# Scaling the scores of heads 0 to 7 in the exponential instead of scaling q

## The chip, the cores and the metric

The kernel runs on one core of a Trainium2 chip. The metric is the device time of one execution in microseconds (us). The engines are TensorE (PE in the rows, its weight loads PEld), VectorE (DVE), ScalarE (ACT), GpSimd (POOL) and SyncE (SP, whose queue issues the transfers here).

## What is computed

Attention over 4 batches of 8 heads (576 tokens, head width 64, causal by blocks of 64 tokens), and two feed-forward layers (width 512, inner width 2048) on its output:

```python
scores = scale * np.matmul(q, k.transpose(0, 1, 3, 2))      # scale = 1 / sqrt(64)
scores = np.where(mask, scores, -1000000000.0)
scores = scores - np.max(scores, axis=-1, keepdims=True)
attn = np.exp(scores)
attn = attn / (np.sum(attn, axis=-1, keepdims=True) + 1e-09)
x = np.matmul(attn, v)
...
h = x @ w_in;  g = np.maximum(0.01 * h, h);  x = g @ w_out
h = x @ w2_in;  g = P(h) / (Q(h) + 1e-06);  out = g @ w2_out
```

## The kernel before

The 32 heads are worked through one by one in one loop. The first eight (`NSF = WHOLE = 8`, the first batch) take plain 32-bit matmuls; from head 8 on q, k, the probabilities and v are split into a high and a low part. While a batch's heads are computed, matmuls of the first layer for the batch before are filled in between (`moe1`), so during heads 0 to 7 there are none; TensorE then has only the heads' own work. Beside all this the weights are converted block by block (`convert`): a block `cs` is loaded by SP, ScalarE (line 174) and GpSimd (178, for the first nine blocks) take its halves apart, VectorE (196) joins them, ScalarE (199) rounds a high part and GpSimd (200) subtracts it.

One head has a row of steps, in an order given by a string (`ORDERS` for head 0, `ORDER0` for heads 1 to 8). Their parts, with lines of the profile:

- Step 1 calls `a1(n + 1)`: for heads 1 to 7 ScalarE multiplies the next head's q (tile `fq`, 64 x 576) by the scale in place (line 272 through the helper at 262).
- Steps x, y, z call `a2_part`: TensorE computes the scores of one or two of the head's five row tiles (308), VectorE takes each row's negated maximum into `nm` (320), ScalarE takes the exponentials with that maximum as bias and the row sums as a second output (326). x is the last row tile (576 keys), y has those of 448 and 320 keys, z those of 192 and 64. Behind the last of them `a2_norm` adds a small number to the sums, takes reciprocals (332, 333) and normalises the five tiles (336, on VectorE in these heads).
- Steps a and b transpose the normalised tiles of the head before (363) and copy them out of PSUM, by ScalarE or VectorE (346).
- Step 4 multiplies the transposed tiles of head n - 2 with v (391, 395); ScalarE casts the result to a high part `xh` (402), VectorE subtracts (403) and copies the last 64 columns (404).

Scores, transposes and products all use one PSUM pool of four buffers (tile `T`), so a matmul group often waits for an exponential or a copy that empties a buffer. The tiles of q and k, and those of the probabilities (`PB`, five for even heads, five for odd ones), are reused too.

Head 0 is an exception already before the change: its q isn't scaled; its maxima are (324), and its exponential has the scale as a factor.

The order of the instructions on SP is the order of the code. On the other engines a scheduler of the framework sets it, by costs of its own, so an instruction less or more can move others. Each engine then works strictly in that order.

Of the kernel before, what the change touches and what calls it, by code (L numbers as in the profile page):

```python
# [14 lines left out]
AF = mybir.ActivationFunctionType  # L15
# [10 lines left out]
def attention_moe_moe_kernel(  # L26
# [15 lines left out]
    B, H, D, S = q.shape  # L42
# [8 lines left out]
    SCALE = 1.0 / float(D) ** 0.5  # L51
# [39 lines left out]
    plain = [  # L91
        [ap.tile([P, S], F32, tag=f"{nm}{j}", name=f"{nm}{j}") for nm in ("fq", "fk")] for j in range(4)
    ]
# [4 lines left out]
    PB = [[ap.tile([P, P * (i + 1)], F32, name=f"PB{e}{i}") for i in range(5)] for e in range(2)]  # L98
# [29 lines left out]
    NSF = 8  # L128
# [105 lines left out]
    def split_tiles(n):  # L234
        e, j = n % 2, (2 * n - NSF) % 4
        for d, nm, i in ((QT, "fq", j), (KH, "fk", j), (QM, "fq", j + 1), (KL, "fk", j + 1)):
            d[e] = ap.tile([P, S], F32R, tag=f"{nm}{i % 4}", name=f"split_{nm}{i % 4}")
        for c, d in enumerate((QM, KL)):
            src = plain[(NSF - 1) % 4][c] if n == NSF else d[1 - e].bitcast(F32)
            cp1("p", d[e][D:P, :], src[D:P, :])  # L240
# [19 lines left out]
    def cp1(eng, out, in_, by=1.0):  # L260
        if eng == "a":
            nc.scalar.activation(out, in_, AF.Copy, scale=by)
        elif eng == "v":
            nc.vector.tensor_scalar(out, in_, by, None, ALU.mult)
        else:
            nc.gpsimd.tensor_scalar(out, in_, by, 1.0, ALU.mult, ALU.mult)

    def a1(n):
        if n < NSF:
            if n > 0:  # L270
                fq = plain[n % 4][0][0:D, :]
                cp1("a", fq, fq, SCALE)
            return
        if n < NSF + 2:
            split_tiles(n)
        e = n % 2
        qs, ks = qk[e][0:D, :], qk[e][D:P, :]
        cp1(E1[0], QT[e][0:D, :], qs, SCALE)
        nc.vector.scalar_tensor_tensor(
            QT[e][D:P, :], qs, SCALE, QT[e][0:D, :].bitcast(F32), ALU.mult, ALU.subtract  # L280
        )
        cp1(E1[2], QM[e][0:D, :], QT[e][0:D, :].bitcast(F32))
        cp1(E1[3], KH[e][D:P, :], ks)
        cp1(E1[4], KH[e][0:D, :], ks)
        (nc.gpsimd if n < NSF + 3 else nc.vector).tensor_tensor(
            KL[e][0:D, :], ks, KH[e][D:P, :].bitcast(F32), ALU.subtract
        )
# [9 lines left out]
    def a2_part(n, tiles, st):  # L297
        e = n % 2
        nm, sm = st
        done = []  # L300
        T = psA.tile([P, 1024], F32, tag="A", name="T")
        for o, i in tiles:
            ln = KEYS[i]
            parts = [(o, 0, max(ln, P))] if i < 4 else [(512 - NH2, 0, NH2), (512, NH2, NH2)]
            for po, c, w in parts:
                if n < NSF:
                    fq, fk = plain[n % 4]
                    nc.tensor.matmul(  # L308
                        T[:, po:po + w], lhsT=fq[:, FIRST[i]:FIRST[i] + P], rhs=fk[:, c:c + w],
                        start=True, stop=True,  # L310
                    )
                    continue
                for lhs, rhs in ((QT, KH), (QM, KL)):
                    nc.tensor.matmul(  # L314
                        T[:, po:po + w], lhsT=lhs[e][:, FIRST[i]:FIRST[i] + P], rhs=rhs[e][:, c:c + w],
                        start=(lhs is QT), stop=(lhs is QM),
                    )
            done.append((i, ln, T[:, parts[0][0]:parts[0][0] + ln]))
        for i, ln, sc in done:
            nc.vector.tensor_reduce(nm[:, i:i + 1], sc, axis=AX.X, op=ALU.max, negate=True)  # L320
        idx = [i for i, _, _ in done]
        c = slice(min(idx), max(idx) + 1)
        if n == 0:
            nc.vector.tensor_scalar(nm[:, c], nm[:, c], SCALE, None, ALU.mult)
        for i, ln, sc in done:
            nc.scalar.activation(  # L326
                PB[e][i][:, 0:ln], sc, AF.Exp, scale=SCALE if n == 0 else 1.0, bias=nm[:, i:i + 1], accum_out=sm[:, i:i + 1]
            )

    def a2_norm(n, sm):  # L330
# [338 lines left out]
    with tc.manual_schedule(engines={mybir.EngineType.SP}):  # L669
# [51 lines left out]
        for n, (b, h) in enumerate(heads):  # L721
# [3 lines left out]
            nm = cp.tile([P, 5], F32, tag="nm", name="nm")  # L725
            sm = cp.tile([P, 5], F32, tag="sm", name="sm")
# [3 lines left out]
            for step, f in zip(steps, fills):  # L730
                if step == "1" and n + 1 < NHD:
                    a1(n + 1)
                elif step == "v":
                    if n >= WHOLE:
                        a1v(n)
                    if n < WHOLE and odd:
                        load_v(p + 1)
                elif step == "4":
                    save_left()
                    apply(n - 2)  # L740
                elif step == "x":
                    a2_part(n, [(0, 4)], (nm, sm))
                elif step == "y":
                    a2_part(n, [(0, 3), (512, 2)], (nm, sm))
                elif step == "z":
                    a2_part(n, [(0, 1), (512, 0)], (nm, sm))
                elif step == "a" and n > 0:
                    if n >= WHOLE and odd and p < NHD // 2 - 1:
                        load_v(p + 1)
                    a3a(n - 1)  # L750
                elif step == "b" and n > 0:
                    a3b(n - 1)
                if step == max("xyz", key=steps.index):
                    a2_norm(n, sm)
                fill(f)
                pace(n, steps.index(step) + 1)
# [90 lines left out]
```

## Time and profile before

| | |
|---|---|
| median of three runs | 1027.13 us (1027.13 to 1029.51) |
| the profiled execution's own time | 1031.21 us |
| its span, first to last instruction | 1029.3 us |
| busy: TensorE, VectorE, ScalarE, GpSimd | 96%, 71%, 65%, 26% of the span |
| granted TensorE clock, mean | 0.991 |

The span is a little shorter than the execution, which also holds what lies before the first and after the last instruction. Busy shares are averages over very different stages: the heads come first, then what is left of the first layer, then the second layer with TensorE at work all the time. A matmul's end is modelled, so a busy TensorE may still be waiting inside.

### The profile page before, as it was taken

The numbers are of one execution on the slowest core, as the hardware profiler recorded it, in microseconds if no ns is written. First come the engines' busy times: TensorE is split into PE (matmuls) and PEld (weight loads), VectorE is DVE, ScalarE is ACT, GpSimd is POOL, SyncE is SP. The second block draws the span as 40 slices with busy tenths as digits, with TensorE's granted clock in tenths as the row PEclk, the third lists the DMA queues.
The fourth block names the chain that finished last, engine by engine and source line by source line (L and its number), as shares of the span: only waits on it lengthen the run. The fifth ranks groups of instructions, "written<-read, shape, count | busy, mean of one in ns | idle before, by whom it ended". The sixth has DMA issues, their size and how long they took to land.

```text
span 1029.3 us, 14577 instructions
## 1 busy us (share of the span) xinstructions
PE 991.0 (96%) x4968; PEld 828.4 (80%) x4968; DVE 731.4 (71%) x1270; ACT 672.8 (65%) x1371; POOL 272.6 (26%) x333
## 2 busy tenths in 40 slices
PE   6989989898999999999999999999999999999997
PEld 4667777787888888888888898888888888888886
DVE  4797767676676676665333234999888888888885
ACT  5778877766566766665554334876766776676675
POOL 5256656554444563532331211000000000000000
PEclk8999999999999999999999999999999999999999
DMA  6457959546454574542865686602102000110010
GB/s 181 134 162 257 305 175 288 184 163 211 128 169 148 161 240 127 177 139 78 280 199 183 209 293 236 254 1 82 42 1 82 21 22 4 37 41 1 1 42 21
DMA packets 94762, 140.95 MB, mean 137 GB/s; under 512 B 10336, under 2 KB 47200, under 8 KB 94688
## 3 DMA queue, kind: packets, MB, share of 16 engines
q1 hardware_dynamic: 94688, 140.02, 42.3%
q8 instruction: 39, 0.64, 0.3%
q14 instruction: 35, 0.29, 0.1%
HBM read 108.53 MB, written 31.46 MB: 136 GB/s over the span
## 4 chain that ended last, share of the span: by engine, by line
PE 77%; ACT 7%; DVE 6%; DMA 5%; issue 3%; POOL 2%; SPq 1%; DVEq 0%; ACTq 0%; POOLq 0%
PE M L480 29%; PE h L581 19%; PE o L635 19%; PE T L363 3%; DMA cs<-in_moe_w_in_dram 3%; PE T L395 3%; PE T L314 2%; ACT PB L326 2%; PE T L308 1%; DVE nm L320 1%; ACT cs L174 1%; DMA xld<-vr 1%; DVE PB L336 1%; DVE pTl L356 1%; ACT cs L180 1%
## 5 line engine op out<-in xcount | busy, mean ns | idle before, releaser
L480 PE MATMUL M<-gh,w1o 128*128 128x512 f32 (+1 forms) x320 | 120.4, 377 | 5.7 <-ACT PB L326 3.2
L480 PE MATMUL M<-gl,w1o 128*128 128x512 f32 (+1 forms) x320 | 120.2, 376 | 0.0
L480 PE MATMUL M<-gh,wl 128*128 128x512 f32 (+1 forms) x320 | 119.3, 373 | 0.0
L326 ACT ACTIVATE PB<-T,nm 128x448 f32<-128x448 f32 (+4 forms) x160 | 83.1, 524 | 43.7 <-DVE nm L320 40.7
L593 ACT ACTIVATE ea<-h,coef 128x512 f32<-128x512 f32 (+1 forms) x80 | 51.7, 646 | 90.8 <-PE h L581 90.7
L490 DVE TENSOR_TENSOR gl<-M,gh 128x512 fp32r<-128x512 f32 (+1 forms) x80 | 50.5, 632 | 68.6 <-ACT M L489 68.6
L581 PE MATMUL h<-x2h,w2h 128*128 128x512 f32 (+1 forms) x240 | 88.3, 368 | 0.5 <-DVE acc L497 0.5
L581 PE MATMUL h<-x2h,w2l 128*128 128x512 f32 (+1 forms) x240 | 88.3, 368 | 0.0
L581 PE MATMUL h<-x2l,w2h 128*128 128x512 f32 (+1 forms) x240 | 88.3, 368 | 0.0
L635 PE MATMUL o<-w2h,g2h 128*128 128x512 f32 x216 | 84.2, 390 | 0.0
L635 PE MATMUL o<-w2l,g2h 128*128 128x512 f32 x216 | 84.2, 390 | 0.0
L635 PE MATMUL o<-w2h,g2l 128*128 128x512 f32 x216 | 84.0, 389 | 0.0
L336 POOL TENSOR_SCALAR PB<-PB,sm 128x448 f32<-128x448 f32 (+4 forms) x120 | 69.9, 604 | 48.9 <-DVE sm L333 48.9
L320 DVE TENSOR_REDUCE nm<-T 128x1 f32<-128x448 f32 (+4 forms) x160 | 71.6, 479 | 14.0 <-PE T L308 10.6
L174 ACT ACTIVATE cs<-cs 128x512 f32<-128x512 f32 x64 | 43.1, 674 | 57.2 <-DMA cs<-in_moe_w_in_dram 36.3
L596 DVE SCALAR_TENSOR_TENSOR ea<-eh,coef,ea 128x512 f32<-128x512 f32 (+1 forms) x80 | 55.7, 696 | 33.5 <-ACT eh L594 32.7
L363 PE MATMUL T<-ident,PB 128*128 128x128 f32 x480 | 67.8, 282 | 10.6 <-ACT PB L326 6.6
L480 PE MATMUL M<-xh,w1i 128*128 128x512 f32 x256 | 74.6, 402 | 2.0 <-ACT xh L412 1.1
L363 PEld LDWEIGHTS T<-ident,PB 128*128 128x128 f32 x480 | 56.9, 145 | 23.4 <-ACT PB L326 5.6
L196 DVE SCALAR_TENSOR_TENSOR cl<-cs 128x512 int32<-128x512 int32 x64 | 52.4, 822 | 31.9 <-ACT cs L180 23.9
L480 PEld LDWEIGHTS M<-gh,w1o 128*128 128x128 f32 x320 | 60.6, 190 | 15.8 <-ACT PB L326 3.9
L480 PE MATMUL M<-xh,wl 128*128 128x512 f32 x256 | 73.0, 401 | 0.0
(128 smaller groups left out, 2533.5 us busy)
## 6 DMA issues: line engine op xcount, KB each, us to landing
wl<-w1l SPq DMA_DIRECT2D x160, 256.0 KB, 2.9
cs<-in_moe_w_in_dram SPq DMA_DIRECT2D x32, 512.0 KB, 5.3
cs<-in_moe_w_out_dram SPq DMA_DIRECT2D x32, 512.0 KB, 5.5
w1l<-cl SPq DMA_DIRECT2D x32, 256.0 KB, 4.9
vr<-in_v_dram SPq DMA_DIRECT2D x16, 256.0 KB, 3.4
w2h<-ch SPq DMA_DIRECT2D x16, 256.0 KB, 3.7
w2l<-cl SPq DMA_DIRECT2D x16, 256.0 KB, 3.9
x2hd<-xo SPq DMA_DIRECT2D x16, 256.0 KB, 2.7
```

What stands on the lines that cost most here:

```text
L174: nc.scalar.activation(hi.bitcast(F32), hi.bitcast(F32), AF.Prelu, scale=2.0 ** -112, alpha=-(2.0 ** 32))
L196: nc.vector.scalar_tensor_tensor(f.bitcast(I32), hi, 3, lo, ALU.logical_shift_left, ALU.bitwise_or)
L320: nc.vector.tensor_reduce(nm[:, i:i + 1], sc, axis=AX.X, op=ALU.max, negate=True)
L326: nc.scalar.activation(PB[e][i][:, 0:ln], sc, AF.Exp, scale=SCALE if n == 0 else 1.0, bias=nm[:, i:i + 1], accum_out=sm[:, i:i + 1])
L336: (nc.vector if n < WHOLE else nc.gpsimd).tensor_scalar(PB[e][i][:, 0:ln], PB[e][i][:, 0:ln], sm[:, i:i + 1], 1.0, ALU.mult, ALU.mult)
L363: nc.tensor.transpose(T[:, c:c + P], PB[e][i][:, kt * P:(kt + 1) * P], ident)
L480: nc.tensor.matmul(T, lhsT=w[:, kk, :], rhs=A[kk][lo], start=(m == 0), stop=(m == 11))
L490: nc.vector.tensor_tensor(gl, T, gh.bitcast(F32), ALU.subtract)
L581: nc.tensor.matmul(h[:, 0:n], lhsT=a, rhs=x, start=(kk == 0 and i == 0), stop=(kk == KD - 1 and i == 2))
L593: nc.scalar.activation(a, h, AF.Abs, scale=coef[:, 4:5])
L596: nc.vector.scalar_tensor_tensor(a, h2, coef[:, 5:6], a, ALU.mult, ALU.add)
L635: nc.tensor.matmul(ob[t], lhsT=a, rhs=w, start=(f == 0 and i == 0), stop=(f == NF - 1 and i == 2))
```

## The change

Heads 1 to 7 are treated as head 0 was: q is left unscaled, the maxima are multiplied by the scale, and the exponential multiplies the scores by it.

```diff
     def a1(n):
         if n < NSF:
-            if n > 0:
-                fq = plain[n % 4][0][0:D, :]
-                cp1("a", fq, fq, SCALE)
             return
...
         c = slice(min(idx), max(idx) + 1)
-        if n == 0:
+        if n < NSF:
             nc.vector.tensor_scalar(nm[:, c], nm[:, c], SCALE, None, ALU.mult)
         for i, ln, sc in done:
             nc.scalar.activation(
-                PB[e][i][:, 0:ln], sc, AF.Exp, scale=SCALE if n == 0 else 1.0, bias=nm[:, i:i + 1], accum_out=sm[:, i:i + 1]
+                PB[e][i][:, 0:ln], sc, AF.Exp, scale=SCALE if n < NSF else 1.0, bias=nm[:, i:i + 1], accum_out=sm[:, i:i + 1]
             )
```

Line numbers behind the first place are lower by three in the changed kernel (326 is 323, 402 is 399). In the rows below `PB_103` to `PB_107` are the five probability tiles of an even head and `PB_108` to `PB_112` those of an odd one, in the order of their row tiles (64, 192, 320, 448, 576 keys).

ScalarE at the start of the program, before:

```order
L670 ACT_TABLE_LOAD
L262 ACTIVATE fq_95<-fq_95 64x576
L262 ACTIVATE fq_97<-fq_97 64x576
L174 ACTIVATE cs<-cs 128x512
L262 ACTIVATE fq_99<-fq_99 64x576
L326 ACTIVATE PB_106,sm<-T,nm 128x448
L326 ACTIVATE PB_105,sm<-T,nm 128x320
L326 ACTIVATE PB_104,sm<-T,nm 128x192
L326 ACTIVATE PB_103,sm<-T,nm 128x64
L326 ACTIVATE PB_107,sm<-T,nm 128x576
L326 ACTIVATE PB_112,sm<-T,nm 128x576
L174 ACTIVATE cs<-cs 128x512
```

The same place with the change:

```order
L667 ACT_TABLE_LOAD
L174 ACTIVATE cs<-cs 128x512
L323 ACTIVATE PB_106,sm<-T,nm 128x448
L323 ACTIVATE PB_105,sm<-T,nm 128x320
L323 ACTIVATE PB_104,sm<-T,nm 128x192
L323 ACTIVATE PB_103,sm<-T,nm 128x64
L323 ACTIVATE PB_107,sm<-T,nm 128x576
L174 ACTIVATE cs<-cs 128x512
L323 ACTIVATE PB_112,sm<-T,nm 128x576
L199 CAST w1i<-cl 128x4x128
L174 ACTIVATE cs<-cs 128x512
L323 ACTIVATE PB_111,sm<-T,nm 128x448
```

The three scalings of q are gone, and the second weight block now stands ahead of head 1's first exponential (`PB_112`).

ScalarE in head 5, before:

```order
L326 ACTIVATE PB_112,sm<-T,nm 128x576
L326 ACTIVATE PB_111,sm<-T,nm 128x448
L326 ACTIVATE PB_110,sm<-T,nm 128x320
L402 CAST xh<-T 64x512
L346 COPY acc<-T 128x896
```

The same place with the change:

```order
L323 ACTIVATE PB_112,sm<-T,nm 128x576
L199 CAST w1o<-cl 128x4x128
L399 CAST xh<-T 64x512
L323 ACTIVATE PB_111,sm<-T,nm 128x448
L323 ACTIVATE PB_110,sm<-T,nm 128x320
L343 COPY acc<-T 128x896
```

The cast of the product with v (`xh`, of head 3) moved ahead of two exponentials; the same happens in head 2.

VectorE at the first maxima of head 6, before:

```order
L336 TENSOR_SCALAR PB_110<-PB_110,sm 128x320
L320 TENSOR_REDUCE nm<-T 128x1 x2
L279 SCALAR_TENSOR_TENSOR split_fq_647<-qk_89,split_fq_647 64x576
L196 SCALAR_TENSOR_TENSOR cl<-cs 128x512
L403 TENSOR_TENSOR xl<-T,xh 64x512
```

The same place with the change:

```order
L333 TENSOR_SCALAR PB_110<-PB_110,sm 128x320
L321 TENSOR_SCALAR nm<-nm 128x1
L317 TENSOR_REDUCE nm<-T 128x1 x2
L276 SCALAR_TENSOR_TENSOR split_fq_658<-qk_89,split_fq_658 64x576
L321 TENSOR_SCALAR nm<-nm 128x2
L196 SCALAR_TENSOR_TENSOR cl<-cs 128x512
```

The two rows of line 321 are new. The first, for x, stands behind the normalisation of head 5 (line 333); the second, for y, behind the split of q for head 8 (line 276).

## Rows read from the trace of the kernel before

**Rows 1.** The page, 40 slices of the span: granted TensorE clock, in tenths.

```profile
PEclk8999999999999999999999999999999999999999
```

**Rows 2.** Chain that ended last, 0 to 260 us: start, us, what.

```profile
30.65 0.68 DVE xl L403
...
44.28 0.60 ACT fq L262
...
55.11 0.59 ACT xh L402
55.71 0.92 ACT acc L346
```

**Rows 3.** Timeline of ScalarE: start, us, instruction, [idle before <-releaser].

```profile
9.32 0.67 ACT L174 ACTIVATE cs<-cs 128x512 f32<-128x512 f32 x1 [1.95 <-DMA cs<-in_moe_w_in_dram]
12.08 0.68 ACT L262 ACTIVATE fq<-fq 64x576 f32<-64x576 f32 x1 [2.09 <-DMA fq<-in_q_dram]
12.67 0.61 ACT L326 ACTIVATE PB<-T,nm 128x448 f32<-128x448 f32 x1
...
13.28 0.51 ACT L326 ACTIVATE PB<-T,nm 128x320 f32<-128x320 f32 x1
...
14.47 0.74 ACT L326 ACTIVATE PB<-T,nm 128x576 f32<-128x576 f32 x1
...
15.19 0.74 ACT L326 ACTIVATE PB<-T,nm 128x576 f32<-128x576 f32 x1
...
43.60 0.68 ACT L174 ACTIVATE cs<-cs 128x512 f32<-128x512 f32 x1 [1.48 <-DMA cs<-in_moe_w_in_dram]
44.19 0.69 ACT L262 ACTIVATE fq<-fq 64x576 f32<-64x576 f32 x1
44.78 0.62 ACT L326 ACTIVATE PB<-T,nm 128x448 f32<-128x448 f32 x1
```

**Rows 4.** Timeline of VectorE.

```profile
8.87 0.16 DVE L324 TENSOR_SCALAR nm<-nm 128x2 f32<-128x2 f32 x1
8.94 0.22 DVE L320 TENSOR_REDUCE nm<-T 128x1 f32<-128x64 f32 x1
...
11.57 0.15 DVE L324 TENSOR_SCALAR nm<-nm 128x1 f32<-128x1 f32 x1
...
33.86 1.57 DVE L336 TENSOR_SCALAR PB<-PB,sm 128x448 f32<-128x448 f32 x5
...
43.20 1.02 DVE L320 TENSOR_REDUCE nm<-T 128x1 f32<-128x448 f32 x2
...
59.59 3.84 DVE L336 TENSOR_SCALAR PB<-PB,sm 128x448 f32<-128x448 f32 x5
...
64.40 0.75 DVE L279 SCALAR_TENSOR_TENSOR split_fq<-qk,split_fq 64x576 fp32r<-64x576 f32 x1
```

**Rows 5.** Timeline of TensorE.

```profile
4.59 6.57 PE L308 MATMUL T<-fk,fq 128*128 128x448 f32 x16 [4.59 <-POOL fk L229]
13.94 2.93 PE L308 MATMUL T<-fk,fq 128*128 128x448 f32 x4 [2.77 <-ACT PB L326]
...
23.11 2.58 PE L308 MATMUL T<-fk,fq 128*128 128x288 f32 x8
...
25.76 2.75 PE L395 MATMUL T<-acc,vr 128*128 128x448 f32 x10
```

**Rows 6.** Stages: length, busy PE, PEld, DVE, ACT, POOL, then PEclk, DMA share, GB/s.

```profile
12.00:14.00 2.00, 0.06 (x1) 0.06 (x1) 0.39 (x1) 1.92 (x6) 0.00 (x0) 0.80 1.09 241
...
23.50:24.00 0.50, 0.50 (x3) 0.38 (x2) 0.50 (x2) 0.30 (x1) 0.12 (x1) 1.00 0.52 86
...
70.00:80.00 10.00, 8.95 (x50) 6.78 (x48) 9.87 (x23) 8.63 (x23) 6.65 (x7) 1.00 0.57 174
```

**Rows 7.** All scalings of q on line 262: duration min/median/max in ns.

```profile
L262 ACT ACTIVATE fq<-fq x7: 670/682/687, 5.2 to 44.2; 64x576 f32<-64x576 f32 x7
```

**Rows 8.** Timeline of GpSimd.

```profile
15.44 0.65 POOL L178 TENSOR_SCALAR cs<-cs 128x512 int32<-128x512 uint32 x1 [4.96 <-DMA cs<-in_moe_w_in_dram]
```

## The prediction

> **What bounds the kernel now.** I looked first at the page's row of the granted TensorE clock over the whole span [rows 1]: nine tenths or more everywhere but in the first slice. TensorE is busy 96% of the span, so most of it is closed to a change that touches no matmul. The edit lives in heads 0 to 7, the first 80 us or so; only there can time be won or lost, and what is won there is kept if the rest follows relative to it.
>
> The second view is the chain that ended last, cut to the first stage [rows 2]. There it isn't TensorE that leads. The chain goes back and forth between casts and copies on ScalarE and small work on VectorE, and a scaling of q appears in it by name at 44.28 us. The reader is to see that the links are short and of many engines: moving one of them by half a microsecond counts only if it stands in this chain.
>
> The third view is the timeline by engine. On ScalarE [rows 3] the scaling of head 3's q starts at 12.08 after 2.09 us of waiting for a DMA, and the five exponentials of head 0, whose first maxima were scaled at 8.87 + 0.16 = 9.03 us [rows 4], stand behind it. On TensorE [rows 5] that shows as an idle stretch of 2.77 us ending at 13.94 with an exponential as releaser. The stages [rows 6] show the price: the granted clock falls from 1.00 to 0.80 in 12 to 14 us, and the next two matmul scores take 2.93 us at the lower level (1.2 GHz); it is back at 2.4 GHz in the second half of 23 to 24 us. The last view is VectorE's fill: 9.87 of 10 us in 70 to 80 us [rows 6].
>
> **Removed: seven scalings of q on ScalarE**, 0.682 us each [rows 7], of which about 0.6 us each is time that a follower waits. Five lie in gaps: ScalarE waits for something else right before or after them, and those are worth nothing. Two are on the chain.
>
> *The first, at 12.08.* Without it ScalarE goes from the first weight block (9.32, next start 0.59 later, as at 43.60 and 44.19) to head 0's exponentials at 9.91 instead of 12.67. The fifth needs the third scaled maximum, 11.57 + 0.15 = 11.72 [rows 4]. TensorE's wait at 13.94 ended 0.66 after the second exponential's start at 13.28; that start becomes 9.91 + 0.61 = 10.52, so the wait ends at 11.18, just as the first group of matmuls ends (4.59 + 6.57 = 11.16). The gap of 2.77 us goes.
> What is late next: the second weight block. GpSimd waits for it until 15.44 [rows 8], and in the new order ScalarE converts it *ahead* of head 1's first exponential, which starts at 15.44 + 0.59 = 16.03, against 15.19 before: 0.84 us later. Behind it come that exponential (0.72), a cast (0.6 as an estimate, like its neighbours), a third block (0.6) and head 1's second and third exponentials at 17.95 and 18.56; head 2's first scores, which need the buffer of these, start at 18.56 + 0.66 = 19.2, where the eight matmuls before started at 23.11 [rows 5].
> Now the clock decides. At 2.4 GHz the eight matmuls take about 2.5 us (2.58 in that group at 23.11, at whose start the clock was just rising), and the product with v that follows 2.75: it ends at 24.4 instead of 25.76 + 2.75 = 28.51, a gain of 4.1. At 1.2 GHz the eight take 5.0 and the product ends at 27.0: a gain of 1.5. TensorE will still wait for the normalisations after 12.6 and for the exponential of 16.03, so I expect part of the stretch at the lower level, and take the middle, **2.8 us** (1.5 to 4.1).
>
> *The second, at 44.28*, 0.60 us on the chain between a weight block that arrived at 43.60 and head 4's exponentials. Their maxima end at 43.20 + 1.02 = 44.22, plus 0.16 for the new scaling 44.38, against 44.78 when the exponentials started [rows 3, 4]: **0.4 us** (0 to 0.6).
>
> **Moved: a copy on ScalarE.** The scheduler, whose costs changed, puts the cast of the attention output (xh, L402 before) of heads 2 and 5 ahead of the exponentials instead of behind them. For head 5 the chain has that cast, 0.59 us from 55.11, and right behind it the copy at 55.71 that the next scores wait for [rows 2]: the cast leaves it, 0.6 us. For head 2 the chain leaves through the subtraction at 30.65 that waits for that cast; it is released about two exponentials earlier, of which I count 0.6. Sum **1.2 us** (0 to 1.4).
>
> **Added: 21 scalings of maxima on VectorE**, three to a head in heads 1 to 7. The records last 0.16 us, but the next instruction starts 0.07 after them (8.87 and 8.94 [rows 4]). I charge 0.07 for the nine of heads 5 to 7, where VectorE is full, **0.65 us**; in the others VectorE has gaps. The bounds are nothing and 21 x 0.16 = 3.4. An exponential with the scale in it costs no more: 576 elements took 0.74 both with it (14.47) and without (15.19) [rows 3].
> The Trainium skill, "VectorE: DVE Perf Modes", section "The DRAIN you can't avoid", says that the next operation doesn't start until the pipeline has emptied, and its section "Rules for kernel authors" asks to minimise the number of operations. This change adds operations, and by that rule each would hold the engine for its record; the rows at 8.87 and 8.94 don't show it for a follower that is independent.
>
> **Displaced:** where the scaling isn't placed right behind its maxima, exponentials wait longer. In head 6 the split of q for head 8 (0.75 us at 64.40 [rows 4]) now comes between them: up to 0.75 + 0.16 lost. Against that, head 5's normalisation of 3.84 us (1.57 in head 2) [rows 4] begins earlier and may meet less work of GpSimd: up to 2.3 gained. These I set to zero and keep for the range. Queue SP's order is unchanged. From head 8 on TensorE's order differs in about 200 rows and then is the same; nothing prices that, and a wrong turn there is worth about a wait like those of 1 to 2 us, both ways.
>
> **Sum:** 2.8 + 0.4 + 1.2 - 0.65 = 3.75 us. The profiled execution took 1031.21 us (span 1029.3), so it would take 1027.5; it stands 4.1 us above the median of the runs, 1027.13, which becomes **1023.4 us**. About 0.3%, 3.1 us, is what a measurement here can tell from nothing.
>
> **Rivals.**
> *The clock stays up* (faster). If TensorE is granted 2.4 GHz through 13 to 23 us and head 5's normalisation escapes: 4.1 + 0.6 + 1.4 + 1.5 (two thirds of the 2.3) = 7.6, 1019.5 us. For it: the gap of 2.77 goes. Against: gaps of 1 to 2 us remain.
> *The second weight block eats the gain* (no difference). It lands at 15.44 whatever ScalarE does, and the new order makes head 1's first exponential wait for it. If the clock falls as before, 1.5 is left; with the moved cast worth nothing, 1.5 + 0.4 - 0.65 = 1.3: 1025.9 us. For it: that wait is sure [rows 8]. Against: the chain before went through scores at the low clock, which start earlier.
> *Each scaling holds VectorE for its record* (no difference): with 18 of heads 2 to 7 at 0.16, 2.9 in place of 0.65, the gain is 1.5 and the time 1025.6 us. This is what the rule of the skill named above would give.
> *Scaled maxima queue behind other work* (slower). VectorE executes in order; if in each of heads 2 to 7 a scaling comes behind one more operation (0.68 to 0.75) and the exponentials stand for it, the price is 6 x (0.7 + 0.16) = 5.2, against the lowest start gain of 1.5: 3.7 lost, 1030.8 us. It decides from about 0.8 us a head on. For it: the order has such a place in heads 2, 3, 4 and 6. Against: in heads 3 and 4 ScalarE has other work there.
> That the change doesn't do what it says is excluded by the order: seven scalings gone, 21 added.
>
> **Chances.** Forecast 0.38; clock stays up 0.12; block eats the gain 0.29; record held 0.05; slower 0.16. So faster by over 0.3% 0.50, within it 0.34, slower 0.16. The range takes in the full clock rival, 1019.5, and goes up past both flat rivals and the unpriced order of heads 8 and 9 to 1029.5.
>
> **What would show it.** Right: head 0's first exponential near 9.9 us, no TensorE gap before 11.2, head 1's first exponential near 16.0, the product with v of head 0 ending between 24.4 and 27.0, vector scalings with followers 0.07 us behind, head 4's exponential straight behind its weight block. Wrong: if that product still ends near 28.5; if exponentials of heads 2 to 7 name scaled maxima as releaser for more than half a microsecond each; or if a gain reached by 80 us is gone by 300 us.

## The result and the profile after

The changed kernel took 1031.7 us (median of 22 runs, 1029.3 to 1036.7), the kernel before in the same job 1027.1 (22 runs, 1023.4 to 1032.4): ratio 1.0051, 95% interval 1.0039 to 1.0063. It is slower by about 5 us; I had forecast 3.7 us less. The profiled execution took 1031.75 us, its span is 1029.8. All line numbers are now 3 lower behind the edit.

**The start came as forecast.** The row of the granted clock has no dent in the first slice any more, where before had an 8 [rows 1]:

```profile
PEclk9999999999999999999999999999999999999999
```

ScalarE goes from the first weight block straight to head 0's exponentials, at 10.48 instead of 12.67 [rows 3]; the second block then stands ahead of head 1's first exponential, at 15.57. Timeline of ScalarE after:

```profile
9.91 0.67 ACT L174 ACTIVATE cs<-cs 128x512 f32<-128x512 f32 x1 [7.90 <-DMA cs<-in_moe_w_in_dram]
10.48 0.61 ACT L323 ACTIVATE PB<-T,nm 128x448 f32<-128x448 f32 x1
...
14.98 0.69 ACT L174 ACTIVATE cs<-cs 128x512 f32<-128x512 f32 x1 [1.86 <-DMA cs<-in_moe_w_in_dram]
15.57 0.73 ACT L323 ACTIVATE PB<-T,nm 128x576 f32<-128x576 f32 x1
```

On TensorE the idle stretch of 2.77 us [rows 5] shrinks to 0.87, and the product with v of head 0 ends at 22.13 + 2.75 = 24.88, not 28.51. Timeline of TensorE after:

```profile
11.75 1.56 PE L305 MATMUL T<-fk,fq 128*128 128x448 f32 x4 [0.87 <-ACT PB L323]
...
19.57 2.50 PE L305 MATMUL T<-fk,fq 128*128 128x288 f32 x8 [1.71 <-POOL cs L178]
21.91 0.38 PE L388 MATMUL T<-acc,vr 128*128 128x128 f32 x2
22.13 2.75 PE L392 MATMUL T<-acc,vr 128*128 128x448 f32 x10
```

**Then the gain melts, head by head.** The product with v of heads 0, 2, 4, 5, 6 and 8 starts at 25.54, 41.59, 59.04, 69.32, 76.28 and 101.89 us before and at 21.91, 39.95, 57.63, 70.91, 78.35 and 104.88 after: 3.6 us ahead, then 1.6, 1.4, and behind by 1.6, 2.1 and 3.0. The worst place is head 6, where after the changed order the split (L276) also stands between the maxima and their scaling. Timeline of VectorE there:

```profile
57.53 3.52 DVE L333 TENSOR_SCALAR PB<-PB,sm 128x448 f32<-128x448 f32 x5
60.97 0.14 DVE L321 TENSOR_SCALAR nm<-nm 128x1 f32<-128x1 f32 x1
61.03 1.00 DVE L317 TENSOR_REDUCE nm<-T 128x1 f32<-128x448 f32 x2
62.06 0.75 DVE L276 SCALAR_TENSOR_TENSOR split_fq<-qk,split_fq 64x576 fp32r<-64x576 f32 x1
62.84 1.41 DVE L321 TENSOR_SCALAR nm<-nm 128x2 f32<-128x2 f32 x1
```

A scaling of two numbers a partition, priced at 0.07, lasts 1.41 us. It has the start and, to 0.02 us, the end of an operation of GpSimd; ScalarE's exponentials wait for it (1.54 us), and for its neighbour behind the normalisation (3.26 us); then TensorE waits 2.66 us. Timelines of GpSimd, ScalarE and TensorE of the same place:

```profile
62.84 1.39 POOL L282 TENSOR_TENSOR split_fk<-qk,split_fk 64x576 fp32r<-64x576 f32 x1 [1.23 <-ACT split_fk L262]
```

```profile
61.22 0.74 ACT L323 ACTIVATE PB<-T,nm 128x576 f32<-128x576 f32 x1 [3.26 <-DVE nm L321]
...
64.29 0.63 ACT L323 ACTIVATE PB<-T,nm 128x448 f32<-128x448 f32 x1 [1.54 <-DVE nm L321]
```

```profile
65.58 0.98 PE L360 MATMUL T<-ident,PB 128*128 128x128 f32 x7 [2.66 <-ACT PB L323]
66.85 4.22 PE L305 MATMUL T<-fk,fq 128*128 128x288 f32 x8 [0.29 <-ACT acc L343]
```

The eight matmuls at 66.85 took 4.22 us, 2.50 in head 0, because the granted clock fell behind the wait: 1.00 up to 66 us, then 0.80 and 0.50, which is 1.2 GHz. Stages after (columns as in [rows 6]):

```profile
58.00:66.00 8.00, 4.94 (x27) 3.37 (x26) 7.06 (x12) 3.22 (x9) 6.28 (x8) 1.00 0.74 238
66.00:68.00 2.00, 1.71 (x9) 1.28 (x7) 1.55 (x5) 1.98 (x4) 0.77 (x2) 0.80 0.00 0
68.00:70.00 2.00, 2.00 (x4) 1.01 (x4) 1.10 (x2) 1.70 (x6) 1.27 (x1) 0.50 0.00 0
70.00:72.00 2.00, 2.00 (x8) 1.25 (x7) 1.53 (x6) 1.24 (x3) 0.00 (x0) 0.85 0.00 0
```

The view of all instructions on the tile nm, 5 to 95 us, shows that this is not one accident: engines stood idle 15.3 us, 11 times, until a scaled maximum was there. Its first row gives the scalings' durations (min/median/max in ns), the second the idle time they ended, the third all that ScalarE's exponentials waited for maxima, scaled or not:

```profile
L321 DVE TENSOR_SCALAR nm<-nm x24: 135/154/1412, 8.9 to 77.1; 128x2 f32<-128x2 f32 x16, 128x1 f32<-128x1 f32 x8
...
  DVE nm L321: 15.3, 11
...
  ACT PB L323: 17.5, 14
```

Exponentials waited for their maxima before the change too, so only the difference counts. The last row in the same view of before:

```profile
  ACT PB L326: 12.7, 11
```

So 4.8 us of these waits are new.

Grouped by shape in the same stretch, only the two-column form is long (behind the bar: busy us, mean ns | idle before):

```profile
L321 DVE TENSOR_SCALAR nm<-nm 128x2 f32<-128x2 f32 x16 | 5.5, 342 | 0.2
...
L321 DVE TENSOR_SCALAR nm<-nm 128x1 f32<-128x1 f32 x8 | 1.2, 146 | 0.1
```

The mean hides that few are held: four of the sixteen last over 0.2 us (1.24 at 17.30, 0.66 at 54.99, 1.41 at 62.84, 0.23 at 77.06), together some 2.9 us more than at 0.16 each.

### The profile page after: what moved, and what is told of

Read it like the earlier page. It is cut to its first block, busy times and chain, and to the rows that moved or that the text cites. A ratio compares the mean times of both kernels' runs of the same rounds, so it can differ in the third digit from the quotient of the medians.

```text
span 1029.8 us, 14598 instructions
## 1 busy us (share of the span) xinstructions
PE 988.2 (96%) x4968; PEld 825.6 (80%) x4968; DVE 741.6 (72%) x1291; ACT 667.5 (65%) x1364; POOL 274.2 (27%) x333
## 4 chain that ended last, share of the span: by engine, by line
PE 69%; ACT 5%; DVE 4%; DMA 4%; issue 3%; POOL 2%; SPq 0%; POOLq 0%; ACTq 0%; DVEq 0%
PE M L477 25%; PE h L578 19%; PE o L632 19%; PE T L360 2%; DMA cs<-in_moe_w_in_dram 2%; PE T L392 1%; PE T L311 1%; ACT PB L323 1%; DMA cs<-in_moe_w_out_dram 1%; DMA xld<-vr 1%; DVE pTl L353 1%; POOL PB L333 1%; DVE nm L317 1%; DVE split_fq L276 1%; ACT pTh L345 1%
## 5 line engine op out<-in xcount | busy, mean ns | idle before, releaser
L360 PEld LDWEIGHTS T<-ident,PB 128*128 128x128 f32 x480 | 54.5, 140 | 28.2 <-ACT PB L323 7.2
L477 PE MATMUL M<-xl,w1i 128*128 128x512 f32 x256 | 71.5, 393 | 1.3 <-DVE xl L410 1.0
```

The source lines that it names most:

```text
L360: nc.tensor.transpose(T[:, c:c + P], PB[e][i][:, kt * P:(kt + 1) * P], ident)
L477: nc.tensor.matmul(T, lhsT=w[:, kk, :], rhs=A[kk][lo], start=(m == 0), stop=(m == 11))
```

## The experiments

The theories, as the runs name them. **A**: the added scalings stand between maxima and exponentials, and GpSimd holds them. **B**: taking the scaling of q away is itself harmful. **C**: TensorE's new order in heads 8 to 10 is the loss. **D**: the loss is the place in VectorE's queue, with other work put in front of the scaling. Times are ratios to the kernel before on the same chip. Several runs use the unscaled maximum as the shift of the exponentials: there the scaling of the maxima is left out, and the quotient is the same but for the 1e-9 added to the sum.

**The halves of the change.** First the removal alone (no scaling of q, none of the maxima, heads 1 to 7):

```diff
-        if n < NSF:
+        if n == 0:
             nc.vector.tensor_scalar(nm[:, c], nm[:, c], SCALE, None, ALU.mult)
```

> The scaling of q stays removed and the exponential keeps the scale, but the maxima of heads 1 to 7 are not scaled (that product is left out, so those heads subtract eight times the maximum before the exponential). TensorE, VectorE and the transfer queue then have the order of the kernel before. Theory A, the 21 vector scalings stand between maxima and exponentials, wait there for GpSimd, and that is the loss: this kernel is faster than the kernel before by 1 to 4 us (1023 to 1026). Theory B, removing the scalings of q itself did harm (the early weight block in front of the exponentials, or a clock that falls elsewhere): as slow as the change, 1030 to 1033. Theory C, the new order of heads 8 and 9 is the loss: no slower than before, 1025 to 1028, and the gain of heads 0 to 3 is kept.

Measured 0.9984 (0.9966 to 1.0002): TensorE's and VectorE's order are those of before, seven operations of ScalarE are gone (one weight cast moved, the cast of the product with v did not), and that is worth 1.6 us (3.5 at the interval's end). Exponentials wait 12.8 us for maxima, as before. B falls; A and C stay, since the scalings and the new order of TensorE are both gone here. Then the addition alone: before, with a scaling by 1.0 of the maxima in heads 1 to 7.

```diff
-        if n == 0:
-            nc.vector.tensor_scalar(nm[:, c], nm[:, c], SCALE, None, ALU.mult)
+        if n < NSF:
+            nc.vector.tensor_scalar(nm[:, c], nm[:, c], SCALE if n == 0 else 1.0, None, ALU.mult)
```

> The kernel before with the vector operation added alone: q is scaled as before, the exponential has no scale, and the maxima of heads 1 to 7 are multiplied by 1.0. TensorE, VectorE and GpSimd have exactly the order of the change. Theory A: slower than the kernel before by 4 to 8 us (1031 to 1035), at least as slow as the change, since it pays for the additions and saves nothing. Theory B: within 3 us of the kernel before. Theory C: slower by about what the change is, 3 to 6 us, whatever the vector operations themselves take.

Measured 1.0092 (1.0066 to 1.0118): the 21 small operations, with the order that the scheduler gives beside them (TensorE's is the changed kernel's), cost 9 us. A second profile of the kernel before was taken beside them:

> The kernel before once more, for a second profile: the one shown took 1031.21 us where the median of its runs is 1027.13. If its three falls of the clock (13, 146 and 242 us) make the difference, a profile of a run near the median shows fewer of them, and the products with v of heads 5 to 12 start earlier than in the first profile.

It took 1025.56 us; head 0's product started at 23.88, not 25.54, head 8's at 99.09, not 101.89. Of the 3.6 us by which the change is ahead at head 0, 1.7 belong to the execution that I had read.

**Another form of the scaling**, with a second tensor (a new constant tile of zeros):

```diff
-            nc.vector.tensor_scalar(nm[:, c], nm[:, c], SCALE, None, ALU.mult)
+            nc.vector.scalar_tensor_tensor(nm[:, c], nm[:, c], SCALE, zero[:, c], ALU.mult, ALU.add)
```

> The change with another form of the same vector operation: a scalar_tensor_tensor that multiplies by the scale and adds a tile of zeros, in place of the tensor_scalar. The order is that of the change on TensorE, ScalarE and GpSimd, and all but the same on VectorE. In the trace of the change four scalings last 0.6 to 1.4 us instead of 0.15, each time beside a GpSimd operation, while the scalar_tensor_tensor operations there keep their length. Theory A: no scaling of maxima lasts over 0.25 us now, head 6's second one included, and the time falls by 1.5 to 4 us against the change (1028 to 1030). Theories B and C: no difference to the change (1030 to 1033), with the scalings short or not.

Measured 1.0118 (1.0094 to 1.0143), scalings still up to 1403 ns. This form is held too: that part of A, as I had it, falls. The extra loss against the changed kernel lies behind the heads (last product with v at 484.79 against 484.15). One more run bears on that: before, plus that tile and the operation that clears it, unused.

```diff
+    zero = const.tile([P, 5], F32, name="zero")
...
+        nc.vector.memset(zero, 0.0)
```

> The kernel before with one more constant tile of five columns (20 bytes a partition) and the operation that clears it; every engine's order is otherwise that of before. The run with the second tensor in the scaling lost its extra 5 us only behind the heads, from about 650 us on. If the shift of the tiles by 20 bytes is the cause: 1.004 to 1.006 of before, and the stretch from 650 us on 4 us or more longer than before's. If it was the operation's form or chance: 0.999 to 1.001.

Measured 1.0049 (1.0028 to 1.0070) with TensorE's order unchanged. From 800 to 980 us TensorE never idles in either, at the full granted clock (1.00), but its matmuls take longer. One group of them, by shape, in the second profile of before, then with the tile (busy us, mean ns):

```profile
L581 PE MATMUL h<-x2h,w2h 128*128 128x512 f32 x83 | 32.3, 389 | 0.0
```

```profile
L582 PE MATMUL h<-x2h,w2h 128*128 128x512 f32 x85 | 33.4, 393 | 0.0
```

From the 3401st to the 4601st of TensorE's 4968 matmul records, the same work in every run, the traces have 275.5 us with the tile (this run and the one with the second tensor) and 272.0 in all the others. So this extra loss is not the form of the scaling.

**The hold by itself.** A kernel with nothing of the computation: VectorE alternates a maximum over PSUM with one small operation, eight times for each of five kinds, first with GpSimd idle, then with GpSimd scaling 128x512 again and again.

```diff
+            nc.vector.tensor_reduce(nm, T, axis=AX.X, op=ALU.max, negate=True)
+            small(kind, x, o)
...
+            nc.gpsimd.tensor_scalar(dst, src, x[:, 0:1], 1.0, ALU.mult, ALU.mult)
```

> No attention and no layers: VectorE alone alternates a maximum over 128x448 of PSUM with one small operation, 8 times for each of five kinds (scale of two columns, scale of one column, scale of two columns plus a second tensor, scale of two columns out of PSUM, reciprocal of two columns), first with GpSimd idle, then with GpSimd scaling 128x512 again and again. Theory A: with GpSimd idle all are near 0.15 us; beside GpSimd the two columns and the two columns plus a tensor grow to up to GpSimd's own duration, mean over 0.4 us, while one column, PSUM and reciprocal stay within 0.05 us of idle. Rival (any small operation of VectorE is slow beside GpSimd): all five grow.

The groups by form (busy us, mean ns):

```profile
L71 DVE TENSOR_SCALAR two_out_busy<-two_in_busy 128x2 f32<-128x2 f32 x8 | 2.8, 348 | 0.0
L75 DVE SCALAR_TENSOR_TENSOR plus_out_busy<-plus_in_busy,zero 128x2 f32<-128x2 f32 x8 | 2.6, 328 | 0.0
L71 DVE TENSOR_SCALAR two_out_idle<-two_in_idle 128x2 f32<-128x2 f32 x8 | 1.3, 159 | 0.0
L79 DVE RECIPROCAL recip_out_busy<-recip_in_busy 128x2 f32<-128x2 f32 x8 | 1.3, 157 | 0.0
L79 DVE RECIPROCAL recip_out_idle<-recip_in_idle 128x2 f32<-128x2 f32 x8 | 1.2, 152 | 0.0
L75 DVE SCALAR_TENSOR_TENSOR plus_out_idle<-plus_in_idle,zero 128x2 f32<-128x2 f32 x8 | 1.2, 149 | 0.0
L77 DVE TENSOR_SCALAR psum_out_idle<-R 128x2 f32<-128x2 f32 x8 | 1.2, 148 | 0.0
L77 DVE TENSOR_SCALAR psum_out_busy<-R 128x2 f32<-128x2 f32 x8 | 1.2, 147 | 0.0
L73 DVE TENSOR_SCALAR one_out_idle<-one_in_idle 128x1 f32<-128x1 f32 x8 | 1.1, 141 | 0.0
L73 DVE TENSOR_SCALAR one_out_busy<-one_in_busy 128x1 f32<-128x1 f32 x8 | 1.1, 137 | 0.0
```

Two columns grow from 159 to 348 ns, two tensors from 149 to 328; reciprocal, PSUM source and one column stay. (The mean of 0.4 I expected was too high: VectorE falls into step with GpSimd, and each hold is the rest of an operation of 691 ns.) The Trainium skill, "SBUF — State Buffer", section "Who interferes with whom", has the rule: VectorE and GpSimd share a pair of ports under an exclusive lock. A copy or scaling of VectorE in a mode that uses both its ports contends for it, and so does an operation with two SBUF inputs beside a GpSimd operation that reads SBUF; whichever issues second blocks until the other is done. A reduction doesn't contend. The trace agrees, at 1.41 us in head 6.

**The hold taken out of the change.** One column per operation, in all heads:

```diff
-            nc.vector.tensor_scalar(nm[:, c], nm[:, c], SCALE, None, ALU.mult)
+            for i in idx:
+                nc.vector.tensor_scalar(nm[:, i:i + 1], nm[:, i:i + 1], SCALE, None, ALU.mult)
```

> The change, with each scaling of the maxima split into operations on one column (35 of 128x1 in place of 21 of 128x2 or 128x1). In the changed kernel's trace the stretched scalings are all of the 128x2 shape (16 in 5 to 95 us, mean 342 ns, up to 1.41 us) and the 8 of 128x1 stay at 146 ns. Theory A (a two-column scaling is held until GpSimd's operation ends, and that hold is the loss): no scaling above 0.2 us, the exponentials' idle time behind scaled maxima falls from about 15 us to under 10 us in this stretch, the first product with v of head 8 starts 3 us or more before the changed kernel's 104.9 us, and the time is 1.000 to 1.002 of before. Theory D (what costs is the place in VectorE's queue, with other work put between the maxima and their scaling): the holds go but the product of head 8 starts at 104 us or later, and the time stays at 1.004 to 1.007.

Measured 1.0014 (0.9997 to 1.0031): 3.8 us of the loss are gone, although VectorE does 16 operations more. But head 0's product started late (25.18), and TensorE's order is that of before, so more than one thing moved. The next run leaves head 0 alone; TensorE's order is that of before here too:

```diff
+            for w in [slice(i, i + 1) for i in idx] if n in (1, 2, 3, 4, 5, 6, 7) else [c]:
+                nc.vector.tensor_scalar(nm[:, w], nm[:, w], SCALE, None, ALU.mult)
```

> The change with the scalings of heads 1 to 7 on one column each; head 0 keeps its two-column scalings, as in the changed kernel. All runs in which head 0 was on one column (or its scalings on ScalarE) started head 0's product at 25.0 to 26.0 us, the changed kernel and its kin at 20.1 to 23.0. If the hold by GpSimd is the loss in the heads and head 0's form the loss at the start: head 0's product at 20.5 to 23 us, head 8's 75.5 to 77 us later (changed kernel 83.0 later), 0.997 to 1.000 of before. If the one-column operations themselves cost 3 us in the heads: head 8's 79 us later or more, 1.001 to 1.003. If the late start came from chance: head 0 at 25 us again.

Measured 1.0019 (0.9993 to 1.0045), in the range that I had given to a price of the operations themselves and above that of the hold alone (0.997 to 1.000). Head 0's product started at 20.75, head 8's at 98.59, 6.3 us ahead of the changed kernel and 77.8 behind head 0's, between my two expectations. Exponentials waited 11.5 us for maxima (17.5 in the changed kernel). Head 6 in its VectorE timeline, with the split still in between, the scaling behind it 0.15 us long and its follower 0.07 behind:

```profile
59.41 0.75 DVE L276 SCALAR_TENSOR_TENSOR split_fq<-qk,split_fq 64x576 fp32r<-64x576 f32 x1
60.20 0.15 DVE L322 TENSOR_SCALAR nm<-nm 128x1 f32<-128x1 f32 x1
60.27 1.82 DVE L196 SCALAR_TENSOR_TENSOR cl<-cs 128x512 int32<-128x512 int32 x1
```

The hold of GpSimd falls on the next operation, for which no exponential waits. TensorE idles 1.15 us where it idled 2.66, and the clock stays up:

```profile
61.36 0.98 PE L361 MATMUL T<-ident,PB 128*128 128x128 f32 x7 [1.15 <-ACT PB L324]
```

```profile
66.00:68.00 2.00, 2.00 (x10) 1.31 (x8) 2.00 (x8) 1.69 (x4) 0.14 (x1) 1.00 0.00 0
68.00:70.00 2.00, 1.95 (x12) 1.43 (x11) 1.97 (x8) 1.95 (x6) 0.00 (x0) 1.00 0.44 132
```

The scalings on ScalarE leave VectorE nothing to be held with, first in all heads, then in all but head 0:

```diff
-            nc.vector.tensor_scalar(nm[:, c], nm[:, c], SCALE, None, ALU.mult)
+            nc.scalar.activation(nm[:, c], nm[:, c], AF.Copy, scale=SCALE)
```

> The change with the scalings of the maxima on ScalarE (21 more operations in front of its exponentials, none on VectorE). Theory A (GpSimd holds VectorE's two-column operation): no hold is left, the exponentials wait only for the reductions, time 0.999 to 1.002 of before. Rival (any operation put between maxima and exponentials costs its own length, wherever it runs): 21 x about 0.2 us of ScalarE on the path, 4 us over e1, 1.002 to 1.004 of before. Both may be weighed against e1 (0.998): the distance is what the step itself costs without GpSimd.

> The change with the scalings of heads 1 to 7 on ScalarE, head 0's on VectorE as in the changed kernel. If any operation between maxima and exponentials costs its own length: 16 or so x 0.2 us on the path, head 8's product 78 us or more behind head 0's, 1.001 to 1.003 of before. If only the hold by GpSimd costs: 75.5 to 77 us, 0.998 to 1.000.

Measured 1.0036 (1.0021 to 1.0050) and 1.0005 (0.9980 to 1.0031), each scaling 0.20 us. The first is what I expected if each operation costs its own length; but its head 0 starts late too (25.17). The second is the cleanest comparison: head 0 and TensorE's order, but for two matmuls, are those of the changed kernel (ScalarE's own order is not), and 4.7 us are gone, uncertain by 2.9. Head 8's product came 78.5 us behind head 0's in it, against 83.0 in the changed kernel and 75.8 in the removal alone. The operation's own length, which I expected to show there, can't be told apart: two runs below, without any scaling of maxima in heads 1 to 7, took 77.7 and 77.8.

All traces together, one execution of each kernel, show the hold apart from the start. From head 0's product to head 7's the five kernels whose two-column scalings stand before the exponentials in all of heads 1 to 7 took 60.1 to 63.4 us (the changed kernel 63.1), the fourteen others 55.1 to 59.1. TensorE's order up to there is the same in all of them but one.

**The hold, off the path.** As the removal alone, but the product is computed into columns nobody reads:

```diff
+        elif n < NSF:
+            nc.vector.tensor_scalar(cab[:, c], nm[:, c], SCALE, None, ALU.mult)
```

> As e1 (maxima of heads 1 to 7 used unscaled as the shift), but the scaling's multiplication is still done by VectorE, into columns that nobody reads: VectorE has the work and may be held by GpSimd, while no exponential waits for it directly. If VectorE's time and its holds are the loss, whoever reads the product: near the changed kernel, 1.003 to 1.006 of before. If the loss is the step put between the maxima and the exponentials: near e1, 0.998 to 1.001, product of head 8 at 97 to 99 us (e1 96.75, changed kernel 104.88).

Measured 1.0005 (0.9983 to 1.0027). VectorE is held even longer than in the changed kernel:

```profile
L323 DVE TENSOR_SCALAR cab<-nm 128x2 f32<-128x2 f32 x14 | 6.5, 461 | 0.2
```

So the time that VectorE loses is not the price: this run is 2.1 us above the removal alone, not clear of the noise, where the changed kernel is 6.9 above it. The hold costs where an exponential stands behind it.

**The order of VectorE.** The split of heads 8 and 9 put behind the last scaling, with two columns, then with one:

```diff
+        with tc.issue_after(scaled[-1].ins) if n <= NSF + 1 else ExitStack():
             nc.vector.scalar_tensor_tensor(
```

> The change, with the split's subtraction of heads 8 and 9 on VectorE put behind the last scaling issued so far (it stood between head 6's last maxima and their scaling, 0.75 us, in front of the 1.41 us hold). Theory D (displaced order is the loss): head 6's last exponentials start 0.7 us or more earlier, the clock does not fall at 66 us, product of head 7 at 83 us or before (changed kernel 84.97), time 1.001 to 1.003 of before. Theory A: the scaling now meets the GpSimd operation anyway or another one; head 7's product within 1 us of the changed kernel's, time 1.004 to 1.006.

> The change with both mendings: scalings on one column, and the split's subtraction of heads 8 and 9 behind the last scaling. If the hold by GpSimd and the displaced order are two losses: 1.0051 less 0.0037 (one column) less 0.0022 (order) is 0.999 of before, head 6's and 7's products within 1 us of e1's when both are counted from head 0's. If both mendings took away the same loss, the hold of 1.41 us in head 6 and what it brought: 1.001 to 1.002, no better than the one-column run.

Measured 1.0029 (1.0007 to 1.0052) and 1.0033 (1.0016 to 1.0050). With two columns the order helps by some 2 us, not clear of the noise. Its timeline shows a reason: the scaling of head 6 now runs at 62.10 in 0.17 us, before GpSimd's operation begins at 62.88. VectorE, then GpSimd:

```profile
62.10 0.17 DVE L324 TENSOR_SCALAR nm<-nm 128x2 f32<-128x2 f32 x1
```

```profile
62.88 1.40 POOL L285 TENSOR_TENSOR split_fk<-qk,split_fk 64x576 fp32r<-64x576 f32 x1 [1.23 <-ACT split_fk L262]
```

With one column there is no hold to escape, and the order gains nothing (1.0014 without it); the 0.999 expected of two separate losses did not come. D is not a loss of its own here, as far as these two runs tell; TensorE's order moved back towards that of before in both, too.

**The order of TensorE.** The four cases of hold and order need two more runs, and these two were meant for them: the holds with TensorE's order of before (head 0 alone on one column), and the new order with holds only in heads 1 and 2.

```diff
+            for w in [slice(i, i + 1) for i in idx] if n in (0,) else [c]:
```

```diff
+            for w in [slice(i, i + 1) for i in idx] if n in (0, 3, 4, 5, 6, 7) else [c]:
```

> The change with the scalings of head 0 alone on one column: VectorE's order differs from the changed kernel's in the first two heads only, heads 1 to 7 keep the two-column scalings, and TensorE's order is that of before (the changed kernel's differs in heads 8 to 10). If TensorE's order carries some 2 us of the loss (the run without scaling and epsilon lost 1.6 us to the one without scaling, the scalar run 2.2 us to the one-column run, each with the new order against the old): 1.0025 to 1.0035 of before, heads 8 to 10 take 36 to 37 us from product to product (changed kernel 38.0). If the holds carry it all: 1.0045 to 1.0055, as the changed kernel.

> The change with scalings on one column in head 0 and heads 3 to 7, two columns in heads 1 and 2: TensorE's order is the changed kernel's, and the holds of heads 3 to 7 are gone. If the holds are worth about 1.7 us and the order 2 us: 1.003 to 1.004 of before, heads 8 to 10 take 38 us. If the order is worth nothing and the holds all: 1.001 to 1.002, as the one-column run (1.0014).

Measured 1.0084 (1.0047 to 1.0121) and 1.0047 (1.0026 to 1.0069), neither where I expected it. And their traces don't have the orders that the two runs were made for. The first has TensorE's order of the changed kernel, the second that of before, in all 4968 matmul records (the two orders differ in 24 of them, from head 7's product on). It is easily seen at that product, where the changed order has one matmul of the first layer (M) between its first two and its last eight. The changed kernel, then the first run, then the second:

```profile
85.70 0.74 PE L477 MATMUL M<-xh,w1i 128*128 128x512 f32 x1
87.19 2.10 PE L392 MATMUL T<-acc,vr 128*128 128x448 f32 x8 [0.75 <-DVE acc L343]
```

```profile
86.92 0.74 PE L478 MATMUL M<-xh,w1i 128*128 128x512 f32 x1
88.40 2.10 PE L393 MATMUL T<-acc,vr 128*128 128x448 f32 x8 [0.75 <-DVE acc L344]
```

```profile
85.03 2.10 PE L393 MATMUL T<-acc,vr 128*128 128x448 f32 x8 [0.53 <-DVE acc L344]
86.89 0.95 PE L478 MATMUL M<-xh,w1i 128*128 128x512 f32 x3
```

So they are no test of C by their times. The traces of all runs are: from head 7's product to head 10's the seven with the changed order (two of them but for two matmuls) took 57.9 to 59.2 us, with holds or without, the ten with the order of before 54.4 to 57.2 (two more have orders of their own). From head 7's product to the last one the two groups overlap: 398.9 to 401.6 and 395.0 to 402.3. C is therefore not refuted: the new order loses about 2.6 us by head 10, and how much of it is left at the end is not shown.

By what they are, the first of the two is the changed kernel with head 0's scalings on one column, the second the one-column run with two columns in heads 1 and 2. Both lie some 3 us above these partners (the first not clear of the noise) and start head 0 late (25.04 and 26.00); the second loses its time behind head 10. Why stays open.

**Fewer small operations.** The removal alone without the 1e-9 in heads 1 to 7; without any scaling, head 0's too; and that without the 1e-9 in heads 1 to 5:

```diff
-        nc.vector.tensor_scalar(sm, sm, 1e-9, None, ALU.add)
+        if n == 0 or n >= 6:
+            nc.vector.tensor_scalar(sm, sm, 1e-9, None, ALU.add)
```

> As e1, and the addition of 1e-9 to the sums is left out too in heads 1 to 7 (each sum holds the term of its own largest score, so the quotient is the same to rounding). It takes 7 small operations of VectorE of 128x5 away, which showed up to 1.3 us beside GpSimd. TensorE's order in heads 8 to 10 is that of the changed kernel, e1's that of before. Theory A: the holds of these 7 go as well, product of head 8 at 96.0 to 96.7 us (e1 96.75), time 0.995 to 0.998 of before. Theory C (the new order of heads 8 to 10 is a loss of its own): 1.5 us or more slower than e1 from head 10 on (e1 133.7 us), time 1.000 or above.

> As e1, with head 0's maxima unscaled too: the exponentials of all eight heads use the unscaled maximum as the shift (the quotient stays the same but for the 1e-9). TensorE's order is that of before. If the removal is worth what the prediction gave the start: 0.997 to 0.999 of before, head 0's product with v at 20.0 to 20.9 us (e1 20.99). If the start waits for the first blocks anyway: within 0.3 us of e1 everywhere, 0.998 to 1.000.

> The run without any scaling of maxima, and the addition of 1e-9 left out in heads 1 to 5 as well; TensorE's order is that of before. If each small operation of VectorE taken from the first heads is worth about 0.14 us: 0.7 us under the run without any scaling (0.999), 0.998 to 0.999 of before. If these additions were hidden: as that run, 0.9985 to 1.0.

Measured 1.0000 (0.9982 to 1.0018), 0.9990 (0.9972 to 1.0008) and 0.9967 (0.9946 to 0.9989). The last is the best of all, better than I expected (0.998 to 0.999): 3.4 us under the kernel before, 8 to 9 under the changed one. The first gains nothing, as I expected under C: it has the changed kernel's order of TensorE, its head 10's product starts 2.7 us behind that of the removal alone, and its time is 1.6 us above it (not clear of the noise).

## Why the prediction was wrong

*Start.* Right by its own steps: exponential at 10.48 (9.9 forecast), head 1's at 15.57 (16.0), the product ending at 24.88 (24.4 to 27.0). But the sum was taken from an execution that stands at 25.54 where a second one of the same kernel stands at 23.88. Against that one the change was 2.0 us ahead, and the removal alone 2.9.

*What the start is worth at the end.* I took it as kept. The removal alone, which has the start and the missing scaling of head 4, is worth 1.6 us (up to 3.5 by its interval) where these two terms came to 3.2. And the one-column run that starts head 0's product at 25.18 is no slower at the end (1.0014) than the one that starts it at 20.75 (1.0019).

*Head 4.* Wrong: its exponentials don't stand straight behind the weight block but wait for scaled maxima until 43.36, 1.58 us.

*Moved.* The cast stands where I saw it in the changed kernel, but no run shows its 1.2 us by itself: the removal alone has ScalarE's order of before there.

*Added.* This step failed. I charged 0.07 for nine operations (0.63, put into the sum as 0.65 us), at most 21 x 0.16 = 3.4, the length of each operation when nothing is in its way. The changed kernel is 1.0051 less 0.9984, 6.9 us, slower than the removal alone. By the runs with one column or on ScalarE (head 0 as in the change: 1.0019, 1.0005), 3.3 to 4.7 us of that is the hold by GpSimd with the wait and the clock behind it. What is left, 2 to 4 us, is not parted: the step itself between maxima and exponentials, VectorE's time, and TensorE's new order ("nothing prices that", the prediction said, and left it out of the sum) may all stand in it. Each part is uncertain by about 3 us. My rows couldn't show the hold: of head 0's scalings [rows 4] the one at 11.57 met an idle GpSimd, the one at 8.87 only the last 0.12 us of a memset. Others could have. The additions of 1e-9 to the sums, just as small, lasted 657 ns on average in 5 to 95 us of the trace before, while the reciprocals behind them took 182:

```profile
L332 DVE TENSOR_SCALAR sm<-sm 128x5 f32<-128x5 f32 x9 | 5.9, 657 | 3.7 <-ACT PB L326 3.6
...
L333 DVE RECIPROCAL sm<-sm 128x5 f32<-128x5 f32 x9 | 1.6, 182 | 0.1
```

*Displaced.* Set to zero; in head 6 the split did come between, and what its timeline shows is not its 0.75 us but that it moved the scaling into GpSimd's operation.

*The rivals.* The slower one had the right place and, with some luck, nearly the time: scaled maxima that queue, 5.2 us in all, 1030.8. I had its reason as other work ahead in the queue; the runs show a hold. It got 0.16 for want of a row with a price above 0.16. "Each scaling holds VectorE for its record" is not borne out: one-column scalings have followers 0.07 us behind, as head 0's had. The rule of the Trainium skill that it came from ("VectorE: DVE Perf Modes", "The DRAIN you can't avoid") shows in no row here; the same paragraph ends by saying that a next operation which isn't held starts earlier, and that is what these followers do.

*What would show it wrong* named the right row: exponentials that name scaled maxima for over half a microsecond each are what the trace shows, from 27.58 us (2.08) to 70.76 (1.03). But it left out what the same row was before: 12.7 us of waiting for plain maxima. Only the 4.8 us on top of that are a sign.

## What to carry to other kernels

Price a small operation not by its shortest record but by the longest of its kind beside the same neighbours: here two columns cost 0.16 us alone and 1.41 beside GpSimd. If it must stand between a reduction and what waits for it, use a form that the other engine did not hold here (one column, a PSUM source), or put it on the engine that waits, or change the algebra so that it isn't needed. A gain at the start of a pipeline is not a gain at its end; check it against a second execution before it goes into a sum. And take a wait only by its difference to the same wait before, and an order only as the trace has it.

## What was new about the hardware

One column or two decides whether VectorE is held: 137 ns against 348 beside GpSimd. The Trainium skill, "VectorE: DVE Perf Modes", section "Mode 2×_2P — use both read ports for one tensor", halves a tensor along its outermost dimension longer than one; a single column has none, which would be the reason. No run here shows that.

A tile of twenty bytes a partition that nobody reads, with the operation that clears it, made the kernel before 0.5% slower: 1200 matmul records of the second layer, with TensorE busy throughout at the full granted clock, took 275.5 us in place of 272.0. That the place of the tiles does it is likely, but was not tried by itself, nor was why.
